# The last batch's second product in seven block products instead of eight, with sums of w_out's blocks made beside four earlier batches

## The chip, the core and the metric

The kernel runs on one core of one Trainium2 chip. The metric is the device time in microseconds of one execution; three executions were timed. The span is the time from the first to the last instruction in the profiled execution.

## What is computed

```python
# per head: q, k, v of (8 batches, 12 heads, 448, 64), fp32
scores = scale * q @ k.T - log(448)
attn   = 1 / (1 + exp(-scores))
x      = (attn @ v) as (8*448, 768)          # heads side by side
# then
h   = x @ w_in                               # 768 x 2048
g   = h - tanh(h)
out = g @ w_out                              # 2048 x 768
```

Everything is fp32 at the edges. Inside, an operand is scaled and split into two fp16 parts (high and low), and a product is three matmuls: high by high, high by low, low by high.

## The kernel before

The program walks over eight batches of 448 tokens, and in each over three kinds of work: attention (`stream`, L506: `scores` L413, sigmoid in `weigh` L434, split in `split_a` L443, times v in `av` L453), the **first product** x @ w_in with the curve g (`moe1`), and the **second product** g @ w_out (`moe2`, L901). PE, ACT, DVE, POOL and, from batch 1 on, SP run in the order in which the program is written. Attention of the next batch is cut into blocks, and `second` (L1161) interleaves them with the second product: a table of positions (`BLOCKS`, `AFTER`, `NORMS7`) says after which step of six matmuls a block, a conversion or a norm comes. All loads and stores go through SP's queue.

Batch 0 also converts the weights, which arrive as fp64 bit patterns: `conv_load` (L154) loads a piece, `conv_sign` and `conv_bits` (L203) make fp32 of it at its `home`, `conv_end` (L207) adds its columns up. w_in comes in 24 pieces, w_out in 32; the last twelve pieces of w_out (the phase "product") are loaded at L172 into tiles `rawo` while the second product of batch 0 already runs. When a half of w_out is there, it is split into fp16 parts in place (`split_w_out`, L334, at L261 to L264).

From batch 3 on (`SEVEN`) the first product is Strassen's: w_in's blocks of 256 x 256 and x's halves are added and subtracted beforehand, and seven products of quarter size take the place of eight (`seven`, L1467: 9 matmuls of 224 columns each, three chunks by three part products). The sums of w_in's blocks were made during batches 1 and 2, lie in DRAM and are streamed through a ring of three buffers (`ring`, `fetch`, L1245). For each k of eight, `Small.moe1` issues `front`, `copy`, `seed`, `cross`, `middle`, `reseed`, `close` and then `square`, `times`, `curve` and `value`, which make g, and `highs` and `lows` (L1452, L1458), which split it. PE does 63 matmuls for a k.

The second product is still the plain one in all batches: for each of three tiles of 128 tokens, 16 chunks of f by three part products by two halves of w_out, 96 matmuls of 384 columns (L921); then the 64 tokens left over, with the two halves side by side in the array (L969, 96 matmuls). ACT and DVE scale the result (L954, L958, L978), and SP stores it (L914). In the last batch no attention is left to interleave.

## Time and profile before

| what | value |
| --- | --- |
| median of 3 runs | 1139.16 us (1138.32 to 1140.37) |
| profiled execution | 1139.2 us |
| its span | 1137.3 us |
| PE busy | 1123.9 us (99%) |
| DVE, ACT, POOL busy | 807.6, 739.7, 216.5 us |
| last batch, first product | from 1028.9 us |
| last batch, second product | from 1079.6 us, with 12 of its matmuls at 1075.9 us |
| last matmul ends | 1132.4 us |

PE, ACT, DVE, POOL and SP are the five instruction queues. "L921" is line 921 of the kernel before. Start times are microseconds from the span's start. PE is busy in all stages; the other engines' shares differ from stage to stage, so what matters is read stage by stage.

### The profile page before, as it was taken

To read this page: it belongs to the slowest core of one execution; us is meant where nothing else is said; L and a number is where in the kernel's file an instruction comes from. 1 tells how busy PE (TensorE), PEld (TensorE's weight loads), DVE (VectorE), ACT (ScalarE), POOL (GpSimd) and SP (SyncE) were. 2 spreads that over 40 slices of the span, in tenths; PEclk is the share of its full clock that TensorE was granted. 3 is DMA by queue.
4 is the path that set the end of the run, shared out by engine and by line. 5 is a ranking of instruction groups with operands and counts; after the bars stand their busy time and mean duration, and the time that the engine had idled before them with its cause. 6 is when DMAs were issued, how large, how long until landed. Compare 5 with 4: busy or idle time off the path is not lost.

```text
span 1137.3 us, 21304 instructions
## 1 busy us (share of the span) xinstructions
PE 1123.9 (99%) x8678; PEld 702.5 (62%) x8678; DVE 807.6 (71%) x1302; ACT 739.7 (65%) x1159; POOL 216.5 (19%) x229
## 2 busy tenths in 40 slices
PE   9999999999999999999999999999999999999998
PEld 2345444555555554569855796559955697559965
DVE  6989699676678787777767686786867777636710
ACT  7987786555886467775676667675676766644610
POOL 0033200014020485310034002320033100330000
PEclk9999999999999999999999999999999999999999
DMA  9992171353222447215622174224622156003301
GB/s 363 404 354 74 29 219 54 83 125 112 75 80 59 141 144 268 73 40 199 236 72 63 51 279 145 63 64 143 246 98 65 43 206 231 17 14 138 128 15 37
DMA packets 64023, 149.28 MB, mean 131 GB/s; under 512 B 18480, under 2 KB 41776, under 8 KB 58800
## 3 DMA queue, kind: packets, MB, share of 16 engines
q1 hardware_dynamic: 63696, 147.55, 38.0%
q8 instruction: 69, 1.13, 0.4%
q10 hardware_dynamic: 224, 0.33, 0.1%
q14 instruction: 34, 0.28, 0.1%
HBM read 119.54 MB, written 28.31 MB: 130 GB/s over the span
## 4 chain that ended last, share of the span: by engine, by line
PE 88%; DMA 4%; DVE 3%; ACT 2%; issue 1%; POOL 1%; SPq 0%; ACTq 0%; DVEq 0%; POOLq 0%
PE po L921 29%; PE ph L1467 16%; PE ph L835 9%; PE acc L463 8%; PE sc L423 8%; PE ph L1047 6%; PE por L969 6%; PE phq L1467 3%; PE php L1467 2%; DMA raw<-moe_w_in 2%; DVE wo L264 1%; ACT a L434 1%; DMA qnn<-q 1%; DVE wi L264 1%; DMA wi<-raw 1%
## 5 line engine op out<-in xcount | busy, mean ns | idle before, releaser
L921 PE MATMUL po<-wo,g 128*128 128x384 f16 x2304 | 389.5, 326 | 1.4 <-DVE g L829 0.7
L921 PEld LDWEIGHTS <-g 128*128 128x128 f16 x2304 | 220.5, 98 | 165.1 <-issue 24.3
L1467 PEld LDWEIGHTS <-wi 128*128 128x128 f16 x2520 | 241.2, 98 | 3.5 <-issue 2.4
L450 DVE SCALAR_TENSOR_TENSOR ahl<-a,ahl 128x896 f16<-128x896 f32 x126 | 156.5, 1254 | 61.7 <-ACT ahl L449 60.3
L434 ACT ACTIVATE a<-sc,nls,rn 128x896 f32<-128x896 f32 x147 | 156.3, 1094 | 50.9 <-PE sc L423 49.5
L1467 PE MATMUL ph<-wi 128*128 128x224 f16 x1890 | 188.5, 259 | 0.1
L494 POOL TENSOR_TENSOR x<-x 128x448 f32<-128x448 f32 x24 | 24.9, 1037 | 488.3 <-ACT x L477 488.3
L835 PE MATMUL ph<-xhl,wi 128*128 128x448 f16 x576 | 109.3, 352 | 0.0
L423 PE MATMUL sc<-Q,K 64*128 64x448 f16 x1008 | 100.8, 353 | 2.4 <-ACT a L434 2.4
L835 PEld LDWEIGHTS <-wi 128*128 128x128 f16 x576 | 56.2, 98 | 52.8 <-issue 0.6
L463 PE MATMUL acc<-ahl,vhl 128*64 128x448 f16 (+1 forms) x864 | 80.6, 356 | 0.0
L449 ACT ACTIVATE ahl<-a 128x896 f16<-128x896 f32 x85 | 79.3, 944 | 0.6
L1047 PE MATMUL ph<-x,wi 128*128 128x448 f32 x192 | 74.5, 541 | 0.0
L423 PEld LDWEIGHTS <-K 64*128 64x128 f16 x1008 | 35.6, 97 | 54.2 <-issue 32.9
L969 PE MATMUL por<-wo,g 128*64 128x384 f16 x768 | 64.9, 327 | 0.0
L463 PEld LDWEIGHTS <-vhl 128*64 128x64 f16 (+1 forms) x864 | 38.4, 108 | 40.2 <-issue 19.8
L1544 ACT ACTIVATE u<-ph,ih 128x896 f32<-128x896 f32 x30 | 30.3, 1009 | 43.7 <-PE ph L1467 43.7
L1047 PEld LDWEIGHTS ph<-x,wi 128*128 128x128 f32 x192 | 35.7, 190 | 33.1 <-issue 31.3
L969 PEld LDWEIGHTS <-g 128*64 128x64 f16 x768 | 42.4, 110 | 22.2 <-issue 4.5
L1458 DVE SCALAR_TENSOR_TENSOR g<-m,Sg,g 128x448 f16<-128x448 f32 x80 | 53.4, 678 | 3.7 <-ACT g L1452 3.7
L958 DVE TENSOR_SCALAR o<-po,iK 128x384 f32<-128x384 f32 x20 | 12.3, 616 | 58.9 <-PE po L921 43.5
L1452 ACT ACTIVATE g<-m,Sg 128x448 f16<-128x448 f32 x80 | 48.9, 660 | 6.9 <-DVE m L1558 5.8
(196 smaller groups left out, 1512.8 us busy)
## 6 DMA issues: line engine op xcount, KB each, us to landing
wi<-set SPq DMA_DIRECT2D x40, 1344.0 KB, 5.9
knn<-k SPq DMA_DIRECT2D x45, 224.0 KB, 2.6
qnn<-q SPq DMA_DIRECT2D x44, 224.0 KB, 2.7
rawo<-moe_w_out SPq DMA_DIRECT2D x22, 384.0 KB, 6.0
out<-o SPq DMA_DIRECT2D x21, 384.0 KB, 2.3
raw<-moe_w_in SPq DMA_DIRECT2D x13, 512.0 KB, 8.1
vn<-v SPq DMA_DIRECT2D x24, 256.0 KB, 3.0
raw<-wi SPq DMA_DIRECT2D x8, 768.0 KB, 8.0
```

The costliest lines, as they stand in the source:

```text
L423: self.nc.tensor.matmul(ps[i * m : (i + 1) * m, h, : self.S], K[i][r, w, c * P : c * P + m], Q[i][r, x, :], start=(n == 0), stop=(n == len ...
L434: self.nc.scalar.activation(a[:, 0], ps[:, :, : self.S], AF.Sigmoid, bias=self.nls, scale=scale)
L449: nc.scalar.activation(A[:, 0], a[:, 0], AF.Copy, scale=A_SCALE)
L450: nc.vector.scalar_tensor_tensor(A[:, 1], a[:, 0], A_SCALE, A[:, 0], op0=ALU.mult, op1=ALU.subtract)
L463: self.nc.tensor.matmul(acc[i][h * D : (h + 1) * D, : self.S], v[k, w, 2 * QT + h if half else h * QT + c], A[k, x, h], start=(n == 0 and ...
L835: self.nc.tensor.matmul(ph, self.wi[:, self.slot(c, k), part, e * P : (e + 1) * P], xhl[c][:, x, :], start=(i == 0), stop=(i == len(prods) ...
L921: nc.tensor.matmul(po[i][:, :H], gs[f // 2][:, x, f % 2, tk * P : (tk + 1) * P], self.wo[:, i * self.NF + 2 * ks[f // 2] + f % 2, w], star ...
L969: nc.tensor.matmul(po[e * D : (e + 1) * D, :H], gs[f // 2][:, x, f % 2, nm:S], self.wo[:, e * self.NF + 2 * ks[f // 2] + f % 2, w], start= ...
L1047: nc.tensor.matmul(ph[:, e, :S], self.fp32(self.wi, self.slot(c, k))[:, 0, e * P : (e + 1) * P], xs[c], start=(c == 0), stop=(c == self.NC ...
L1452: self.nc.scalar.activation(high, src, AF.Copy, scale=self.Sg)
L1458: self.nc.vector.scalar_tensor_tensor(lows[i], srcs[i], self.Sg, highs[i], op0=ALU.mult, op1=ALU.subtract)
L1467: self.nc.tensor.matmul(out, w[:, c, part, left], self.xblock(c, x, right), start=start and i == 0, stop=i == len(prods) - 1, skip_group_c ...
```

## The change

In the last batch (`ACROSS = 7`) the second product is made transposed, out.T = w_out.T @ g.T, and by Strassen's seven products (`across2`). w_out's blocks are the weights, g is what streams, 224 columns (half the tokens) at a time. The six row blocks of 128 of out.T are taken in three pairs; each pair takes seven products, each of eight k by three part products, 24 matmuls. The first matmul of product 1 is 448 columns wide. For k 0 to 4 products 4, 3 and 1 of all pairs come first, then the order of `LAST7`. The result is stored transposed, and the host turns it round.

The operands are sums and differences of blocks:

- of w_out: `conv_end` stores each of the 32 converted pieces to DRAM in batch 0. In batches 3 to 6, 24 units (six in each batch, at the positions of `UNITS7`) each load four fp32 blocks of 128 x 128 of them, make five more by adding (`late_add`, POOL), split all seven (`late_split`, ACT and DVE, on 256 and 640 columns) and store the parts (`late_store`). In the last batch 21 transfers of 512 KB (`late_fetch`) bring them back, 13 before or while the first product ends, eight as places come free.
- of g: `late_sums` makes, for each k, one addition on 448 columns and three on 224; on POOL for k 0 to 6, on DVE for k = 7. `late_parts` splits four blocks (896 columns) and three (672 columns), where `highs` and `lows` split twice 448.

g of the last batch lies where w_out was; the tile of g of the batches before it becomes one tile, `gall`, and takes the fetched sums.

```diff
+    PAIRS = ((0, 1), (3, 4), (2, 5))
+    LAST7 = (
+        (0, 4, ""), (0, 3, "c"), (1, 4, ""), (1, 3, "c"), (0, 1, "s"), (2, 4, ""), (2, 3, "c"), (1, 1, "s"),
+        (0, 5, ""), (2, 1, "s"), (0, 2, "r"), (1, 5, ""), (1, 2, "r"), (0, 7, ""), (0, 6, "po"), (2, 5, ""),
+        (2, 2, "r"), (1, 7, "p"), (2, 7, "p"), (1, 6, "o"), (2, 6, "o"),
+    )
+    LEFT7 = {1: 2, 2: 1, 3: 5, 4: 6, 5: 0, 6: 3, 7: 4}
+    RIGHT7 = {1: 4, 2: 2, 3: 0, 4: 1, 5: 3, 6: 5, 7: 6}
+    FILL7 = 3
+    EXTRA7 = {5: (7, 8), 6: (9, 10)}
+    TAIL7 = (1, 1, 1, 1)
+    BLOCKS7 = (4, 7, 11, 14, 14, 14, 19, 22, 25, 25, 25, 30, 34, 37, 37)
+    LATE = (3, 4, 5, 6)
+    UNITS7 = (2, 5, 7, 10, 13, 15, 18, 22, 25, 29, 31, 34, 38, 41, 45)
...
+    def conv_end(self, p):
+
+        super().conv_end(p)
+        kind, r, i, n = p["piece"]
+        if kind == "out":
+            self.nc.sync.dma_start(
+                self.late_raws[r // 2][:, r % 2, i * n : (i + 1) * n], self.home(kind, r, i)
+            )
...
+    def late_load(self, n, i):
+
+        d, p = divmod(n, self.NB)
+        da, db = self.PAIRS[d]
+        u = n, self.late_home(i)
+        raw = u[1][0]
+        src = self.late_raws[p].rearrange("p f (b n) -> p (f b) n", n=P)
+        self.nc.sync.dma_start(raw[:, 0], src[:, 6 + da])
+        self.nc.sync.dma_start(raw[:, 1], src[:, db])
+        self.nc.sync.dma_start(raw[:, 2:], src[:, da : 6 + db + 1 : 6 + db - da])
+        return u
+
+    def late_add(self, u):
+
+        G = self.nc.gpsimd
+        w, t = u[1][:2]
+        G.tensor_tensor(t[:, :2], w[:, :2], w[:, 2:], op=ALU.add)
+        G.tensor_tensor(t[:, 2], w[:, 2], w[:, 3], op=ALU.add)
+        G.tensor_tensor(t[:, 3], w[:, 1], w[:, 2], op=ALU.subtract)
+        G.tensor_tensor(t[:, 4], w[:, 0], w[:, 3], op=ALU.subtract)
+
+    def late_split(self, u):
+
+        nc = self.nc
+        w, t, high, low = u[1]
+        for src, at in ((w[:, 2:], slice(5, 7)), (t, slice(0, 5))):
+            nc.scalar.activation(high[:, at], src, AF.Copy, scale=self.So)
+            nc.vector.scalar_tensor_tensor(low[:, at], src, self.So, high[:, at], op0=ALU.mult, op1=ALU.subtract)
+
+    def late_store(self, u):
+
+        n, (_, _, *parts) = u
+        d, p = divmod(n, self.NB)
+        for x in range(2):
+            self.nc.sync.dma_start(self.late_sets[d][:, :, p, x], parts[x])
...
+    def late_fetch(self, at):
+
+        if self.late_order:
+            d, n = self.late_order.pop(0)
+            self.late_at[d, n] = at
+            self.nc.sync.dma_start(self.late_ring(at), self.late_sets[d][:, self.LEFT7[n]])
...
+    def late_sums(self, m, G):
+
+        h = self.half
+        t = self.tp.tile([P, 3, h], F32, name="gt", tag="t")
+        q, p = m[:, 0], m[:, 1]
+        G.tensor_tensor(t[:, 1:].rearrange("p b n -> p (b n)"), p, q, op=ALU.add)
+        G.tensor_tensor(t[:, 0], p[:, :h], p[:, h:], op=ALU.add)
+        G.tensor_tensor(q[:, :h], q[:, :h], p[:, h:], op=ALU.subtract)
+        G.tensor_tensor(q[:, h:], q[:, h:], p[:, :h], op=ALU.subtract)
+        return t
+
+    def late_parts(self, m, t, g, which):
+
+        pairs = ((m.rearrange("p a (b n) -> p (a b) n", b=2), slice(0, 4)), (t, slice(4, 7)))
+        for i in which:
+            src, at = pairs[i]
+            self.nc.scalar.activation(g[:, 0, at], src, AF.Copy, scale=self.Sg)
+            self.nc.vector.scalar_tensor_tensor(
+                g[:, 1, at], src, self.Sg, g[:, 0, at], op0=ALU.mult, op1=ALU.subtract
+            )
...
+        def product(d, n, ps=every):
+            q, p = banks[d]
+            out = {1: p[:, :h], 2: q[:, h:], 3: q[:, :h], 4: q[:, h:], 5: q[:, :h], 6: p[:, h:], 7: p[:, :h]}[n]
+            at = self.late_at[d, n]
+            w = self.late_ring(at)
+            right = self.RIGHT7[n]
+            for k in ps:
+                for part, x in ((0, 0), (0, 1), (1, 0)):
+                    start = n in (1, 4) and k == 0 and (part, x) == (0, 0)
+                    wide = 2 if start and n == 1 else 1
+                    nc.tensor.matmul(
+                        p if wide == 2 else out,
+                        w[:, k, part],
+                        gs[k][:, x, right : right + wide],
+                        start=start,
+                        stop=k == self.NB - 1 and (part, x) == (1, 0),
+                        skip_group_check=True,
+                    )
+                count[0] += 1
+                if count[0] % 2 == 0:
+                    yield 1
+            if k == self.NB - 1:
+                self.late_fetch(at)
...
+        def copy(d):
+            sums[d] = c = self.tp.tile([P, 4, h], F32, name="c", tag="t")
+            nc.scalar.activation(c[:, :2].rearrange("p b n -> p (b n)"), banks[d][0], AF.Copy)
+            V.tensor_tensor(c[:, 2], c[:, 0], c[:, 1], op=ALU.add)
+
+        def seed(d):
+            c = sums[d]
+            V.tensor_tensor(c[:, 3], banks[d][1][:, :h], c[:, 2], op=ALU.add)
+
+        def reseed(d):
+            q, p = (t.rearrange("p (b n) -> p b n", b=2) for t in banks[d])
+            V.tensor_tensor(p, sums.pop(d)[:, 3:4].to_broadcast([P, 2, h]), q, op=ALU.subtract)
+            o = self.op.tile([P, 2, h], F32, name="oq", tag="o", bufs=2)
+            nc.scalar.activation(o, q, AF.Copy, scale=iK)
+            rows = self.rows7(d)
+            nc.sync.dma_start(to[rows[0], h:], o[:, 0])
...
+        def out(d, i):
+            o, p = sums[d], banks[d][1]
+            V.tensor_scalar(o[:, i], p[:, i * h : (i + 1) * h], iK, None, op0=ALU.mult)
+            nc.sync.dma_start(to[self.rows7(d)[i], i * h : (i + 1) * h], o[:, i])
+
+        if b + 1 == self.B:
+            for d in range(3):
+                if d:
+                    both = self.ps.tile([P, 2, 512], F32, name="poa", tag="sc", bufs=2)
+                    banks[d] = [both[:, i, : self.S] for i in range(2)]
+                else:
+                    banks[d] = [self.mm(name) for name in ("poq", "pop")]
+                for n in (4, 3, 1):
+                    yield from product(d, n, early)
+            for d, n, after in self.LAST7:
+                yield from product(d, n, rest if n in (4, 3, 1) else every)
+                for f in after:
+                    {"c": copy, "s": seed, "r": reseed, "p": lambda d: out(d, 0), "o": lambda d: out(d, 1)}[f](d)
...
+        def late_tail():
+            square(last)
+            times(last)
+            curve(last)
+            self.late_parts(*rest.pop(last - 2), (1,))
+            value(last)
+            m, g = ms[last][1], self.gs[last]
+            rest[last] = m, self.late_sums(m, V), g
+            for k in (last - 1, last):
+                self.late_parts(*rest[k], (0, 1))
+            yield 1
+            yield 1
 
...
+            m, g = ms[k - 1][1], self.gs[k - 1]
+            if late:
+                rest[k - 1] = m, self.late_sums(m, nc.gpsimd), g
+                if k > 1:
+                    self.late_parts(*rest[k - 2], (0,))
             close(k)
...
+            if late:
+                middle(k + 1)
+                reseed(k + 1)
+                if k > 1:
+                    self.late_parts(*rest.pop(k - 2), (1,))
...
+            if late:
+                self.late_fetch(k - 1)
+                for n in self.EXTRA7.get(k, ()):
+                    self.late_fetch(n)
...
+        if b in self.LATE:
+            n = 3 * self.NB // len(self.LATE)
+            at = (b - self.LATE[0]) * n
+            made = self.late_units(at, at + n)
+            events += [(p, lambda: next(made)) for p in self.UNITS7]```

How the order of the work moves. First DVE in the first product of the last batch, for one k in the steady state; before (`L1515` seed, `L1558` value, `L1550` times, `L1458` the two splits, `L1529` reseed):

```order
L1515 TENSOR_TENSOR ph<-ph,cp 128x224
L1558 SCALAR_TENSOR_TENSOR m<-u,m 128x896
L1550 SCALAR_TENSOR_TENSOR m<-ph,ihk,u 128x896
L1458 SCALAR_TENSOR_TENSOR g<-m,Sg,g 128x448
L1529 TENSOR_TENSOR ph<-cp,ph 128x448
L1458 SCALAR_TENSOR_TENSOR g<-m,Sg,g 128x2x224
```

and now, with the same steps at `L1779`, `L1822`, `L1814` and `L1793`, and `L1407` in `late_parts`:

```order
L1779 TENSOR_TENSOR ph<-ph,cp 128x224
L1822 SCALAR_TENSOR_TENSOR m<-u,m 128x896
L1407 SCALAR_TENSOR_TENSOR wo<-m,Sg,wo 128x896
L1814 SCALAR_TENSOR_TENSOR m<-ph,ihk,u 128x896
L1793 TENSOR_TENSOR ph<-cp,ph 128x448
L1407 SCALAR_TENSOR_TENSOR wo<-gt,Sg,wo 128x672
```

The two splits are wider, the first of them now stands ahead of `times`, and both belong to a k one earlier than before. POOL, which had no work in a first product, now does this for each k there (`late_sums`):

```order
L1395 TENSOR_TENSOR gt<-m 128x448
L1396 TENSOR_TENSOR gt<-m 128x224
L1397 TENSOR_TENSOR m<-m 128x224
L1398 TENSOR_TENSOR m<-m 128x224
```

Between `value` on DVE and the splits two rows later there is now POOL's work. Second, SP's queue in batch 0, where the last pieces of w_out are loaded (`rawo<-moe_w_out`), from the seventh to the twelfth of them; before:

```order
L172 DMA rawo<-moe_w_out 128x384
L357 DMA vn<-v 128x512
L172 DMA rawo<-moe_w_out 128x384 x2
L347 DMA knn<-k 128x448
L172 DMA rawo<-moe_w_out 128x384
L347 DMA qnn<-q 128x448
L357 DMA vn<-v 128x384
L172 DMA rawo<-moe_w_out 128x384 x2
```

and now, with the stores of converted pieces (`late_127<-wo` and so on, L1284):

```order
L173 DMA rawo<-moe_w_out 128x384
L1284 DMA late_127<-wo 128x384
L358 DMA vn<-v 128x512
L1284 DMA late_128<-wo 128x384 x2
L173 DMA rawo<-moe_w_out 128x384 x2
L1284 DMA late_129<-wo 128x384
L348 DMA knn<-k 128x448
L1284 DMA late_129<-wo 128x384
L173 DMA rawo<-moe_w_out 128x384
L348 DMA qnn<-q 128x448
L358 DMA vn<-v 128x384
L173 DMA rawo<-moe_w_out 128x384 x2
```

The tenth load now stands behind the store of the sixth of the twelve pieces (the second of the two `late_129` rows), which waits until DVE has converted that piece.

## Rows read from the trace of the kernel before

**Rows 1.** The page's first lines: the span; of each engine the busy time, its share of the span and its instructions; and GB/s that the DMA engines moved in each of 40 equal slices.

```profile
span 1137.3 us, 21304 instructions
PE 1123.9 (99%) x8678; PEld 702.5 (62%) x8678; DVE 807.6 (71%) x1302; ACT 739.7 (65%) x1159; POOL 216.5 (19%) x229
...
GB/s 363 404 354 74 29 219 54 83 125 112 75 80 59 141 144 268 73 40 199 236 72 63 51 279 145 63 64 143 246 98 65 43 206 231 17 14 138 128 15 37
```

**Rows 2.** All waits of PE for another engine from 430 us to the end: who waited for whom, us in total, times, longest.

```profile
PE sc L423 <- ACT a L434: 1.5, 1, 1.5
```

**Rows 3.** The chain of waits in the last batch (1000 us to the end): start us, us, what. The lines of L1467 are the first product, those of L921 and L969 the second.

```profile
1039.49 0.19 PE php L1496
1049.16 8.62 PE ph L1467 x90
...
1075.90 1.95 PE po L921 x12
...
1079.58 44.85 PE po L921 x276
1124.43 7.94 PE por L969 x96
...
1132.39 0.62 DVE orem L978
```

**Rows 4.** Windows: stretch, length, then busy us (and instructions) of PE, PEld, DVE, ACT and POOL, granted clock, share of the DMA engines, GB/s. The first is the second product of batch 3 with attention of batch 4 in it, the second the first product of batch 7.

```profile
558.60:640.00 81.40, 81.40 (x671) 44.27 (x670) 57.36 (x92) 61.22 (x102) 21.65 (x23) 1.00 0.24 72
...
1028.80:1079.60 50.80, 50.78 (x521) 49.69 (x520) 33.37 (x58) 26.44 (x44) 0.00 (x0) 1.00 0.39 141
```

**Rows 5.** Groups of instructions by line from 900 to 1137 us, shapes kept in the row: line, engine, operation, out<-in, shapes, count | busy us, mean ns of one | idle before.

```profile
L1515 DVE TENSOR_TENSOR ph<-ph,cp 128x224 f32<-128x224 f32 x12 | 4.8, 397 | 6.8 <-ACT cp L1511 6.8
L1558 DVE SCALAR_TENSOR_TENSOR m<-u,m 128x896 f32<-128x896 f32 x16 | 17.5, 1091 | 5.0 <-ACT u L1554 5.0
L1550 DVE SCALAR_TENSOR_TENSOR m<-ph,ihk,u 128x896 f32<-128x896 f32 x12 | 13.8, 1151 | 10.6 <-ACT u L1544 10.6
L1529 DVE TENSOR_TENSOR ph<-cp,ph 128x448 f32<-128x448 f32 x12 | 7.6, 629 | 6.9 <-PE ph L1467 4.2 <-ACT cp L1525 2.7
L1458 DVE SCALAR_TENSOR_TENSOR g<-m,Sg,g 128x448 f16<-128x448 f32 x32 | 21.4, 678 | 1.5 <-ACT g L1452 1.5
L1393 DVE SCALAR_TENSOR_TENSOR wi<-wi,Sx 128x672 f16<-128x672 f32 x3 | 2.7, 914 | 1.0 <-ACT wi L1390 1.0
L1452 ACT ACTIVATE g<-m,Sg 128x448 f16<-128x448 f32 x32 | 19.6, 660 | 2.7 <-DVE m L1558 2.3
L449 ACT ACTIVATE ahl<-a 128x896 f16<-128x896 f32 x11 | 10.4, 946 | 0.1
L1390 ACT ACTIVATE wi<-wi,Sx 128x672 f16<-128x672 f32 x3 | 2.5, 850 | 3.5 <-DVE Sx L757 3.5
L1525 ACT ACTIVATE cp<-ph 128x224 f32<-128x224 f32 x12 | 4.3, 358 | 6.6 <-PE ph L1467 5.6 <-DVE ih L765 1.0
```

**Rows 6.** The timeline of POOL at three places: start us, us, instruction, shapes. At 176.80 us an addition on 448 columns, at 574.80 us one on 224, and at 586.18 us two instructions on 448.

```profile
176.80 1.14 POOL L503 TENSOR_TENSOR x<-x,x 128x448 f32<-128x448 f32 x1 [9.97 <-ACT x L492]
...
574.80 0.65 POOL L1369 TENSOR_TENSOR wi<-x,x 128x224 f32<-128x224 f32 x1
...
586.18 1.10 POOL L494 TENSOR_TENSOR x<-x 128x448 f32<-128x448 f32 x1 [8.27 <-ACT x L477]
587.36 1.87 POOL L503 TENSOR_TENSOR x<-x,x 128x448 f32<-128x448 f32 x1
```

**Rows 7.** The timeline of DVE: two splits in a row that meet those two, and one that meets no work of POOL.

```profile
586.53 3.65 DVE L450 SCALAR_TENSOR_TENSOR ahl<-a,ahl 128x896 f16<-128x896 f32 x2
...
592.16 1.08 DVE L450 SCALAR_TENSOR_TENSOR ahl<-a,ahl 128x896 f16<-128x896 f32 x1
```

**Rows 8.** Batch 0, where the last pieces of w_out come in. The window from 170 to 180 us (columns as in rows 4), two of PE's waits between 30 and 230 us, three rows of SP's timeline, one of DVE's and two of ACT's.

```profile
170.00:180.00 10.00, 10.00 (x69) 4.79 (x68) 9.50 (x23) 9.51 (x18) 1.14 (x1) 1.00 0.24 82
PE po L921 <- DVE g L829: 0.7, 1, 0.7
PE po L921 <- DVE wo L264: 0.6, 1, 0.6
161.89 0.33 SPq L347 DMA_DIRECT2D knn<-k  x1
162.45 0.33 SPq L172 DMA_DIRECT2D rawo<-moe_w_out  x1
164.97 1.99 SPq L172 DMA_DIRECT2D rawo<-moe_w_out  x2
162.76 0.56 DVE L203 SCALAR_TENSOR_TENSOR wo<-rawo,stb 128x384 uint32<-128x384 uint32 x1
166.82 1.01 ACT L187 ACTIVATE stb<-rawo 128x384 f32<-128x384 f32 x2
172.03 0.57 ACT L187 ACTIVATE stb<-rawo 128x384 f32<-128x384 f32 x1 [0.38 <-DMA rawo<-moe_w_out]
```

**Rows 9.** DMA issues over the span: what, queue, count, KB each, median us from issue to landing.

```profile
wi<-set SPq DMA_DIRECT2D x40, 1344.0 KB, 5.9
out<-o SPq DMA_DIRECT2D x21, 384.0 KB, 2.3
set<-wi SPq DMA_DIRECT2D x48, 64.0 KB, 2.0
out<-orem SPq DMA_DIRECT2D x15, 96.0 KB, 2.2
```

More of the change, by code (lines that the diff above doesn't have):

```diff
@@ L47 @@
     SUMS = 1.0
+    ACROSS = 7
     NORMS = (3, 5, 7)
@@ L1483, in moe1 @@
         ix, bound = st
+        late = b >= self.ACROSS
+        rest = {}
+        if late:
+            self.late_at = {}
+            first = [(d, n) for d in range(3) for n in (4, 3, 1)]
+            self.late_order = first + [(d, n) for d, n, _ in self.LAST7 if n not in (4, 3, 1)]
         base = (b - self.SEVEN) * self.NB
```

167 lines of the change are left out of this document (149 added, 18 removed).

## The prediction

> **What bounds the kernel now.** I read the page's first lines, then PE's waits, then the chain of waits of the last batch, then windows of the stages that the change touches, and at the end single instructions. The page shows PE busy for 1123.9 of 1137.3 us [rows 1], and PE's waits say that this is no average over good and bad stages: from 430 us to the end PE waited for another engine once, for 1.5 us [rows 2]. The chain of the last batch accordingly runs through PE alone, apart from the last two instructions: the first product, then 288 matmuls of 384 columns, then 96 of the rest [rows 3]. So in the last batch time is PE's columns, and a change is worth what it takes off PE, less what it makes PE wait. Batch 0 is the exception: from 170 to 180 us DVE and ACT are both busy for 95% of the time, and PE waits for them (0.7 and 0.6 us are two such waits) [rows 8]. There the conversion of w_out sets the pace, and whatever delays it can come out at the end.
>
> The sum is made against the profiled execution, 1139.2 us, which stands 0.04 us above the median of the runs. About 0.2% of it, 2.3 us, is what a measurement of this kernel tells from no change.
>
> **What the change takes off PE.** Removed: 1.95 + 44.85 + 7.94 = 54.74 us [rows 3]. Added: three pairs by seven products by eight k by three part products, 504 matmuls of 224 columns with 128 x 128 fp16 weights. The first product runs just that shape: 90 in a row took 8.62 us, 95.8 ns each [rows 3]. 504 x 95.8 ns = 48.28 us. Three of them are 448 columns wide; such a one took 0.19 us [rows 3], so 3 x 0.094 = 0.28 us more, 48.56 us in all. **Saved: 6.18 us.** Seven eighths would have given 6.8 us; the short matmuls give part of it back, though the rest of 64 tokens was already dear.
>
> **The end.** After the last matmul DVE scaled 384 columns in 0.62 us [rows 3]; now it is 224 columns, for which a read of PSUM took 0.40 us [rows 5]. Saved: 0.22 us. The last store is 112 KB; stores of 96 and 384 KB landed in 2.2 and 2.3 us [rows 9], so nothing changes there.
>
> **The last batch's first product: DVE and ACT.** PE spends 63 x 95.8 ns = 6.04 us on a k. DVE's work for it was seed 0.40, value 1.09, times 1.15, reseed 0.63 and two splits of 0.68 [rows 5], 4.63 us. The splits become one of 896 columns, 1.08 us when POOL is quiet [rows 7], and one of 672, 0.91 us [rows 5]: 5.26 us, still under 6.04. ACT's two splits go from 1.32 us to 0.95 + 0.85 = 1.80 us [rows 5]; ACT was busy for 26.44 of 50.80 us there [rows 4], and eight times 0.48 us is 3.8 us more. Neither would bind. The order also helps: the wide split now stands ahead of times, and behind times only reseed is left before close of the next k needs it.
>
> **The last batch's first product: POOL.** This is the term that I trust least. POOL did nothing in a first product (0.00 us) [rows 4]; now it adds 448 columns once (1.14 us) and 224 three times (0.65 us) [rows 6] for each k, 3.09 us. POOL and DVE get in each other's way: at 586 us two DVE splits that take 1.08 us alone took 3.65 us together while POOL ran, and POOL's addition of 448 columns, which starts at 587.36 us among them, took 1.87 instead of 1.14 us [rows 6, 7]. 1.10 us of POOL, 1.08 of DVE, 1.14 of POOL and 1.08 of DVE, one behind the other, make 4.4 us, and from 586.18 to 590.18 us 4.0 passed: they took turns, with some overlap at each change. Which of DVE's instructions are met so these rows do not say, so I bound it. If all five groups are met, DVE needs 5.26 + 3.09 = 8.35 us for a k, 2.31 over PE's time, and over seven k that is 16.2 us; that end is the rival below. If only the three that read two tiles of SBUF are met, as the split at 586 us does (value 1.09, splits 1.08 and 0.91), the turns add to 3.08 + 3.09 = 6.17 us against 6.04: just full, and with the overlap at each change just under. times, seed and reseed read PSUM on one side. Below zero it can't go, since nothing is taken away there. I take **0.5 us**, near the second case: what is met at 586 us is an instruction that reads SBUF twice.
>
> The Trainium skill has a rule here that speaks against this change (SBUF — State Buffer, section "SBUF: two separate sides"): the pair of SBUF ports that DVE and GpSimd share is a lock for a whole instruction, and besides 2-port modes it is a DVE instruction with two SBUF inputs that takes it. The rows at 586 us agree as far as they go (3.65 us for two that take 1.08 alone). By the rule alone, with no overlap at the changes, 7 x (6.17 - 6.04) = 0.9 us would stand in the place of the 0.5.
>
> **The seam between the products.** g of k = 7 comes from late_tail behind close. Its DVE work after the last close: times 1.15, a split 0.91, value 1.09, the sums of k = 7 (one 448 and three 224 columns, at most 0.63 + 3 x 0.40 by the nearest additions), four splits 2 x (1.08 + 0.91) [rows 5, 7], together 8.9 us, and about 1 us before them on ACT. PE has 117 of its 135 early matmuls for it, 11.2 us, and reads the second half of k = 7 only some 45 matmuls later. No charge. The 13 places fetched ahead hold 13 x 0.5 = 6.8 MB; with the 141 GB/s of that stage [rows 4] this makes some 275 GB/s, where a slice of this trace moved 404 [rows 1]. A transfer of 1344 KB lands in 5.9 us [rows 9]; the eight refills have over 10 us each. No charge.
>
> **Batches 3 to 6.** A unit costs ACT about 0.36 + 0.85 us and DVE 0.40 + 0.91 (by the rows of 224 and 672 columns, for 256 and 640) [rows 5], POOL at most 4 x 0.65. Six units: ACT 61.22 + 7.3 = 68.5 of 81.40 us, DVE 57.36 + 7.9 = 65.2, POOL 21.65 + 15.6 = 37.3 [rows 4]. The DMA engines were busy for 24% and get 4.2 MB more in 81 us. The two ends are nothing and all of DVE's work, 4 x 7.9 = 31 us. I take **nothing**: PE has not one wait there [rows 2] while DVE and ACT idle for 24 and 20 us. If that cover is gone at a few places, the rival below gives the price.
>
> **Batch 0.** 32 stores go into SP's queue. Where the conversion sets the pace, the tenth of the last twelve loads went out at 162.45 us; it now stands behind the store of a piece whose DVE instruction starts at 162.76 and takes 0.56 us [rows 8]. With 0.4 us for the store's issue that is 163.7 us, 1.3 us later. ACT starts on this piece at about 167.3 us (the second of the two at 166.82) [rows 8], 4.8 us after the old issue, so ACT waits about as long as the load is late, and all behind it with it. The next pair goes out at 164.97 us, after that; its last piece was already waited for (0.38 us) [rows 8]. Ends: nothing, if DVE's queue has enough to do meanwhile, and twice the delay, 2.6 us, if the store traffic slows the loads as well. I take **1.0 us**, most of one delay, since both engines are 95% busy.
>
> **The sum.** 1139.2 - 6.18 - 0.22 + 0.5 + 0 + 1.0 = **1134.3 us**.
>
> **Rivals.** (a) The forecast, between 1132.8 (no charge) and 1135.5: for it speaks that PE is the only bound in the last batch and that every price is of the same shape in the same kernel. Chance 0.60. (b) Both charges larger: 2.6 us in batch 0 and about 1 to 3 us of POOL's turns: 1136.4 to 1138.4. For it: both places are full by the sums above. Chance 0.17, most of it still faster than 1136.9. (c) **Slower:** POOL's sums hold DVE up in all it does, the first product of the last batch becomes DVE's: 8.35 us for a k, 16.2 us in all, 1139.2 - 6.4 + 1.0 + 16.2 = 1150.0 us. It decides from the point where DVE's time for a k passes 6.04 + 5.4 / 7 = 6.81 us, that is 1.55 us of waiting for a k. Against it: only one kind of instruction is seen to wait. Chance 0.07. (d) The units' work hits attention in batches 3 to 6: if one in four of the 24 units puts its DVE time of 1.31 us on PE, 7.9 us, 1142.2 us. Against it: the idle time above. Chance 0.09. (e) The change does not bring what it says: weights come late, or the matmuls run slower than in the first product (at 108.6 ns each, 54.74 / 504, nothing is left). One transfer of up to 5.9 us in the open gives 1140.2. Chance 0.07.
>
> **How the numbers follow.** The time is that of (a). The range 1132.2 to 1140.2 us goes half a microsecond below the case without charges, and up to (e); it holds (a), (b) and (e), 0.84, and leaves out (c) and (d). Faster by over 0.2% (below 1136.9): (a) and most of (b), 0.74. Within 0.2%: the rest of (b) and half of (e), 0.10. Slower: (c), (d) and a little of (e), 0.16.
>
> **What would show it.** PE's second product in the last batch as 504 matmuls in 48.6 us without a wait; one k of the first product still 6.04 us, with DVE at 87% or more and POOL at half; POOL's additions stretched, and value and the splits too, but not times; no new wait of PE in batches 3 to 6; in batch 0 the second product's end some 1 us later. I am wrong if PE waits in the last batch's first product for reseed (close late), or if 224 columns take more than 96 ns.

## The result: slower, 1145.28 against 1139.16 us

The changed kernel takes 1145.28 us (1144.22 to 1146.15, five runs), the kernel before 1139.16 us: ratio 1.0053, 95% interval 1.0038 to 1.0068. Forecast were 1134.3 us and a gain. The profiled execution took 1144.22 us. Its page, first lines (columns as in [rows 1]), and all waits of PE from 430 us on (as in [rows 2]):

```profile
span 1142.3 us, 22173 instructions
PE 1119.9 (98%) x8798; PEld 720.3 (63%) x8798; DVE 886.7 (78%) x1368; ACT 769.4 (67%) x1210; POOL 345.1 (30%) x353
```

```profile
PE po L925 <- DVE o L962: 3.9, 6, 0.9
PE acc L464 <- ACT tn L376: 3.7, 3, 1.2
PE sc L424 <- ACT a L435: 1.0, 1, 1.0
PE por L973 <- ACT o L958: 1.0, 3, 0.3
```

PE has less to do than before (1119.9 us against 1123.9) and waits more. The `sc` wait comes ahead of batch 3 and stood there before; the other three rows are 8.6 us, and the rest of the loss below is in gaps that this view does not list. Where it arises, the starts of the first products tell, in the two profiles:

| stage | before | after | difference | forecast |
| --- | --- | --- | --- | --- |
| to the first product of batch 3 | 507.80 | 508.58 | +0.78 | +1.0 |
| batches 3 to 6 | 520.99 | 531.41 | **+10.42** | 0 |
| batch 7, to its last matmul's end | 103.6 | 97.7 | -5.9 | -5.7 |
| behind it | 5.0 | 4.7 | -0.3 | -0.2 |

Batch by batch the 10.42 us are 3.23, 2.98, 2.86 and 1.35, all of it in the second products. The windows of the same work in the second product of batch 3, before and after, and of the first product of batch 7, after (columns as in [rows 4]):

```profile
560.90:639.80 78.90, 78.90 (x655) 42.67 (x654) 55.93 (x90) 58.84 (x99) 21.65 (x23) 1.00 0.23 71
561.80:643.80 82.00, 79.24 (x655) 43.61 (x653) 71.40 (x102) 64.74 (x110) 45.99 (x47) 1.00 0.44 120
...
1040.00:1090.40 50.40, 50.38 (x526) 50.13 (x525) 36.22 (x55) 27.98 (x43) 25.19 (x24) 1.00 0.69 256
```

DVE was busy for 55.9 us before, now for 71.4: 15.5 us more where 7.9 were forecast. POOL was busy for 24.3 us more, where at most 15.6 were forecast. In batch 7 the view of waits lists none for PE. What happens in batch 3, on three engines; the first fence is the timeline of DVE, the second POOL's, the third PE's (start us, us, instruction):

```profile
573.14 1.22 DVE L451 SCALAR_TENSOR_TENSOR ahl<-a,ahl 128x896 f16<-128x896 f32 x1
574.57 1.53 DVE L451 SCALAR_TENSOR_TENSOR ahl<-a,ahl 128x896 f16<-128x896 f32 x1 [0.21 <-ACT ahl L450]
576.08 1.29 DVE L1339 SCALAR_TENSOR_TENSOR lo<-wi,so,wo 128x256 f16<-128x256 f32 x1
577.30 1.28 DVE L1339 SCALAR_TENSOR_TENSOR lo<-wo,so 128x640 f16<-128x640 f32 x1
578.50 0.60 DVE L962 TENSOR_SCALAR o<-po,iK 128x384 f32<-128x384 f32 x1
```

```profile
572.58 0.83 POOL L1331 TENSOR_TENSOR wo<-wi 128x128 f32<-128x128 f32 x1
573.78 1.38 POOL L495 TENSOR_TENSOR x<-x 128x448 f32<-128x448 f32 x1 [0.36 <-ACT x L478]
575.23 1.86 POOL L504 TENSOR_TENSOR x<-x,x 128x448 f32<-128x448 f32 x1
577.06 0.83 POOL L1626 TENSOR_TENSOR wi<-x,x 128x224 f32<-128x224 f32 x1
```

```profile
578.26 0.34 PE L925 MATMUL po<-wo,g 128*128 128x384 f16 x1
579.16 3.90 PE L925 MATMUL po<-wo,g 128*128 128x384 f16 x23 [0.56 <-DVE o L962]
```

PE can go on with the next tile of 128 tokens only when DVE has read the old one (`o`). A unit's two splits, at place 15, stand just ahead of `o` in DVE's queue. Alone they take 0.48 and 0.88 us; here 1.29 and 1.28, and `ahl` (attention's split) ahead of them 1.22 and 1.53 instead of 1.08, because POOL works almost without a pause from 567.14 to 582.24 us, first on two units' additions, then on the sums of x. The sums of x alone, which were there before, are most of the splits' stretch: in x1 below, without the units' additions, the same two took 2.10 us together (574.82 us on DVE), here 2.50. Over batches 3 to 6 the units' splits took 3.6 us more than in x1, the instructions of `ahl` 18 us more.

The second kind of wait starts on POOL; `tn` is a step of the next head's norms. ACT's timeline:

```profile
607.24 0.49 ACT L1338 ACTIVATE wi<-wi,so 128x256 f16<-128x256 f32 x1
610.33 0.83 ACT L1338 ACTIVATE wi<-wi,so 128x640 f16<-128x640 f32 x1 [2.59 <-POOL wi L1331]
611.06 0.25 ACT L376 ACTIVATE tn<-pbn,tiny 128x6 f32<-128x6 f32 x1
```

The wide split of the fifth unit waits 2.59 us for POOL's additions, which stand behind five sums of x; `tn` stands behind the split, attention behind `tn`, and PE waits 1.24 us for it at 611.36 us.

### The profile page after: what moved, and what is told of

Its sections match the earlier page's. It is cut to its first block, busy times and chain, and to the rows that moved or that the text cites. A ratio compares the mean times of both kernels' runs of the same rounds, so it can differ in the third digit from the quotient of the medians.

```text
span 1142.3 us, 22173 instructions
## 1 busy us (share of the span) xinstructions
PE 1119.9 (98%) x8798; PEld 720.3 (63%) x8798; DVE 886.7 (78%) x1368; ACT 769.4 (67%) x1210; POOL 345.1 (30%) x353
## 3 DMA queue, kind: packets, MB, share of 16 engines
q8 instruction: 70, 1.15, 0.4%
## 5 line engine op out<-in xcount | busy, mean ns | idle before, releaser
L925 PE MATMUL po<-wo,g 128*128 128x384 f16 x2016 | 343.6, 326 | 5.5 <-DVE o L962 3.9
L925 PEld LDWEIGHTS <-g 128*128 128x128 f16 x2016 | 192.3, 98 | 152.0 <-issue 30.1
L451 DVE SCALAR_TENSOR_TENSOR ahl<-a,ahl 128x896 f16<-128x896 f32 x126 | 166.6, 1339 | 41.7 <-ACT ahl L450 40.2
L435 ACT ACTIVATE a<-sc,nls,rn 128x896 f32<-128x896 f32 x147 | 155.8, 1090 | 38.2 <-PE sc L424 36.8
L424 PE MATMUL sc<-Q,K 64*128 64x448 f16 x1008 | 101.0, 353 | 3.3 <-ACT a L435 3.3
L1328 POOL TENSOR_TENSOR wi<-wi 128x256 f32<-128x256 f32 x12 | 12.2, 1018 | 285.0 <-DMA wi<-late 212.4
L464 PE MATMUL acc<-ahl,vhl 128*64 128x448 f16 (+1 forms) x864 | 80.6, 356 | 3.7 <-ACT tn L376 3.7
L450 ACT ACTIVATE ahl<-a 128x896 f16<-128x896 f32 x85 | 79.2, 943 | 0.6
L424 PEld LDWEIGHTS <-K 64*128 64x128 f16 x1008 | 35.6, 97 | 55.2 <-issue 33.4
L464 PEld LDWEIGHTS <-vhl 128*64 128x64 f16 (+1 forms) x864 | 39.3, 108 | 43.2 <-issue 23.3
L495 POOL TENSOR_TENSOR x<-x 128x448 f32<-128x448 f32 x24 | 27.7, 1155 | 115.7 <-ACT x L478 115.7
L973 PE MATMUL por<-wo,g 128*64 128x384 f16 x672 | 56.9, 327 | 1.0 <-ACT o L958 1.0
L1808 ACT ACTIVATE u<-ph,ih 128x896 f32<-128x896 f32 x30 | 30.2, 1005 | 40.1 <-PE ph L1724 40.1
L1814 DVE SCALAR_TENSOR_TENSOR m<-ph,ihk,u 128x896 f32<-128x896 f32 x30 | 34.5, 1150 | 23.2 <-ACT u L1808 23.2
L1822 DVE SCALAR_TENSOR_TENSOR m<-u,m 128x896 f32<-128x896 f32 x40 | 44.1, 1102 | 10.1 <-ACT u L1818 10.0
L1676 POOL TENSOR_TENSOR wsq<-wsq 128x768 bf16<-128x768 bf16 (+1 forms) x16 | 20.7, 1295 | 101.0 <-PE wl L219 60.1
## 6 DMA issues: line engine op xcount, KB each, us to landing
wi<-set SPq DMA_DIRECT2D x40, 1344.0 KB, 5.9
rawo<-moe_w_out SPq DMA_DIRECT2D x22, 384.0 KB, 5.4
out<-o SPq DMA_DIRECT2D x18, 384.0 KB, 2.4
```

The lines of the kernel that those rows point to most:

```text
L424: self.nc.tensor.matmul(ps[i * m : (i + 1) * m, h, : self.S], K[i][r, w, c * P : c * P + m], Q[i][r, x, :], start=(n == 0), stop=(n == len ...
L435: self.nc.scalar.activation(a[:, 0], ps[:, :, : self.S], AF.Sigmoid, bias=self.nls, scale=scale)
L450: nc.scalar.activation(A[:, 0], a[:, 0], AF.Copy, scale=A_SCALE)
L451: nc.vector.scalar_tensor_tensor(A[:, 1], a[:, 0], A_SCALE, A[:, 0], op0=ALU.mult, op1=ALU.subtract)
L464: self.nc.tensor.matmul(acc[i][h * D : (h + 1) * D, : self.S], v[k, w, 2 * QT + h if half else h * QT + c], A[k, x, h], start=(n == 0 and ...
L925: nc.tensor.matmul(po[i][:, :H], gs[f // 2][:, x, f % 2, tk * P : (tk + 1) * P], self.wo[:, i * self.NF + 2 * ks[f // 2] + f % 2, w], star ...
```

## The experiments

The excess below is that of batches 3 to 6 over the 520.99 us of before, from the starts of the first products in each kernel's profile. Of six kernels there is one execution only; for them the excess and the waits carry the argument, and not the time.

| kernel | us | ratio, 95% interval | excess |
| --- | --- | --- | --- |
| changed | 1145.28 | 1.0053 (1.0038 to 1.0068) | 10.4 |
| x1, no sums | 1132.82 | one execution | 0.0 |
| x2, no DVE split | 1134.09 | one execution | 0.9 |
| x3, neither | 1134.26 | one execution | 1.1 |
| x6, sums unread | 1139.70 | one execution | 7.0 |
| x5, no sums, split twice | 1169.92 | one execution | 36.1 |
| y1, sums on DVE | 1167.67 | one execution | 33.5 |
| x4, moved | 1151.64 | 1.0119 (1.0090 to 1.0147) | 16.0 |
| y5, three early | 1148.12 | 1.0074 (1.0061 to 1.0087) | 14.1 |
| z1, y5 without stores | 1148.25 | 1.0067 (1.0054 to 1.0080) | 15.9 |
| z2, y5, POOL's queue | 1147.67 | 1.0068 (1.0055 to 1.0081) | 15.0 |
| w1, two early | 1156.92 | 1.0158 (1.0137 to 1.0178) | 23.7 |
| w2, two early, old places | 1160.50 | 1.0178 (1.0164 to 1.0192) | 27.6 |
| w3, seven in batch 6 | 1162.95 | 1.0215 (1.0201 to 1.0229) | 28.1 |
| w4, stores later | 1141.03 | 1.0013 (1.0003 to 1.0023) | 8.1 |
| w5, split at 28 | 1143.93 | 1.0036 (1.0023 to 1.0048) | 9.8 |
| w6, decoupled | 1139.36 | 1.0005 (0.9996 to 1.0014) | 6.5 |
| w7, decoupled, 36 | 1139.89 | 1.0006 (0.9997 to 1.0016) | 6.0 |
| w8, additions at 28 | 1142.03 | 1.0024 (1.0014 to 1.0033) | 9.3 |

**Which work of a unit costs.** x1:

```diff
 def late_add(self, u):
-    (POOL's four additions)
+    pass
 ...
-for src, at in ((w[:, 2:], slice(5, 7)), (t, slice(0, 5))):
+for src, at in ((w[:, 2:], slice(5, 7)), (w[:, 2:3].to_broadcast([P, 5, P]), slice(0, 5))):
```

> The changed kernel without POOL's additions in the units of batches 3 to 6: the wide split reads one loaded block five times over instead of the five sums, so loads, splits and stores are as before and what is stored is not the sums. The changed kernel's batches 3 to 6 (from the start of one first product to the next) are together 10.4 us longer than before (135.2, 135.0, 134.8 and 126.4 us against three times 132.0 and 125.1). Theory A (POOL's additions and DVE's instructions take turns, and that is what makes DVE late): the excess falls below 2 us, PE's waits for o on DVE and for tn on ACT go, DVE's split of ahl is back at about 1.24 us from 1.37; time about 1136. Theory B (the splits alone overfill DVE): the waits for o stay, about 4 us, and only the three waits of 1.2 us for tn behind an ACT split that waits for POOL go; excess 5 to 7 us, time about 1141. Theory C (traffic of the loads and stores): nothing changes, 1145.

x2 leaves out the line of `nc.vector` in `late_split` and stores `parts[0]` twice; x3 does both.

> The changed kernel without the two DVE splits of each unit; the high parts are stored in the place of the low ones. POOL's additions, ACT's splits, loads and stores stay. Theory A: the additions still stretch attention's own instructions on DVE (17 us over batches 3 to 6 for the two kinds of ahl alone) and still come late for ACT, so the three waits for tn stay (3.7 us) and some of those for o; excess 4 to 6 us, time about 1140. Theory B: with 43 us of DVE work gone the waits for o go and only those for tn stay; excess 4 us or less, time about 1139. Theory C: nothing changes, 1145.

> The changed kernel with neither the additions nor the DVE splits in the units; ACT's splits, loads and stores stay, and what is stored is not the sums. Theories A and B: batches 3 to 6 take what they took before (excess under 1 us), the time is about 1135, and what is left against 1134.3 is batch 0's. Theory C: as the changed kernel, 1145.

x1 is as theory A has it: batches 3 to 6 take 520.98 us, and PE does not wait in them. But x2, where A expected 4 to 6 us, comes out at 0.9 (0.8 of it a wait for a late `wi`, a transfer of the ring). So neither A nor B alone: either half of a unit's cost fits, both together don't. Of traffic (C) no more than such late transfers is seen. The second product of batch 3, window in x1, then in x2, and the two splits of x1 ahead of `o`:

```profile
560.80:639.70 78.90, 78.90 (x655) 42.70 (x654) 65.38 (x102) 65.30 (x111) 25.33 (x23) 1.00 0.46 126
561.40:640.30 78.90, 78.90 (x655) 42.73 (x654) 60.26 (x90) 65.49 (x111) 39.95 (x47) 1.00 0.46 126
574.82 2.10 DVE L1334 SCALAR_TENSOR_TENSOR lo<-wi,so,wo 128x256 f16<-128x256 f32 x2 [0.37 <-ACT wo L1333]
```

DVE's busy time goes from 55.9 (before) over 65.4 (x1, no wait) to 71.4 us (changed): 9.5 us are the splits, 6.0 us are POOL's additions showing up in DVE's time (4.3 us without the splits, in x2). x5 asks whether the source matters. On top of x1:

```diff
-            nc.vector.scalar_tensor_tensor(low[:, at], ...)
+            for _ in range(2):
+                nc.vector.scalar_tensor_tensor(low[:, at], ...)
```

> As the kernel without sums (POOL's additions left out, the wide split reads a loaded block), but each DVE split of a unit is issued twice, so that what is stored is not the sums: DVE gets some 36 us more over batches 3 to 6, as much as it loses by POOL's turns and by the stretched splits in the changed kernel (65 - 36 = 29 us, by busy time). If DVE's time just ahead of o is what counts, from whatever source, PE waits for o again, 0.5 to 1.5 us at the places 16 and 32, and batches 3 to 6 take 4 to 12 us more than before: 1137 to 1145. If POOL's turns and late sums themselves are needed, no wait comes back: 1133 to 1135.

The waits for `o` came back far larger, 3.2 and 2.6 us at the two places of each batch (DVE's timeline, then PE's; the four splits are one row):

```profile
577.38 4.07 DVE L1335 SCALAR_TENSOR_TENSOR lo<-wi,so,wo 128x256 f16<-128x256 f32 x4
581.38 0.60 DVE L962 TENSOR_SCALAR o<-po,iK 128x384 f32<-128x384 f32 x1
```

```profile
582.04 5.21 PE L925 MATMUL po<-wo,g 128*128 128x384 f16 x23 [3.17 <-DVE o L962]
```

So DVE's time ahead of `o` is enough, without POOL's additions. It is more time than theirs, though: over batches 3 to 6 DVE was busy for 370.4 us before, 408.8 in x1, 436.7 in the changed kernel and 454.8 here, 46.0 us over x1 where the additions make it 27.9. The excess is three times the upper end of what was expected. Part of that is PE's clock: behind six of the eight waits it fell (23 matmuls take 5.21 us here, 3.90 in the changed kernel's row above).

x6 keeps POOL's additions, but the splits read as in x1:

> The changed kernel with POOL's additions made as before, but the wide split reads a loaded block five times over, so that nobody waits for the sums and what is stored is not the sums. It parts the two ways in which the additions can cost: that they take turns with DVE (the waits for o stay, 0.5 to 0.9 us at two places of each batch, about 4 us in all), and that ACT's split waits for them with tn behind it (1.2 us in each of three batches, which goes here). Both at work: 1137 to 1141. Turns alone: still 1142 or more. Lateness alone: 1133 to 1135.

Both at work: the waits for `tn` are gone, those for `o` stay, and the excess is 7.0. By difference, from one profile each, 7.0 of the 10.4 us are POOL's turns with DVE, 3.4 us ACT's wait for late sums. PE's waits in x6:

```profile
PE po L925 <- DVE o L962: 4.0, 4, 1.2
PE por L973 <- ACT o L958: 1.1, 3, 0.4
```

These are 5.1 us; the other 1.9 us is in gaps that this view does not list. y1 takes POOL out of it (`G = self.nc.vector` in `late_add`):

> The changed kernel with the units' sums on DVE instead of POOL: about 0.35 + 3 x 0.17 = 0.86 us for a unit, 21 us in all (worked out from 0.62 us for 448 and 0.30 us for 224 columns on DVE in the last batch's late_tail), in the place of POOL's additions with their turns. If DVE's sum of work decides, wherever it comes from, DVE gains 21 us and loses about 25 us of stretch, and the excess of batches 3 to 6 stays at 5 to 10 us: 1141 to 1145. If it is the turns and POOL's lateness alone, the waits go as without the sums: 1133 to 1136.

DVE's sum of work decides, and it is worse than expected: the excess is 33.5 us. The additions were priced at 0.35 and 0.17 us; they take 0.42 and 0.28 us on DVE alone and 0.66 to 0.75 us beside POOL's sums of x in batch 3 (577.96 to 580.62 us), and they stand ahead of the splits and `o`. PE waits 24.0 us for `o`, in eight places.

**Whether other places have room.** x4:

```diff
-    UNITS7 = (2, 5, 7, 10, 13, 15, 18, 22, 25, 29, 31, 34, 38, 41, 45)
+    UNITS7 = (2, 5, 7, 10, 13, 17, 18, 22, 25, 33, 34, 38, 40, 43, 45)
```

> The changed kernel with six of the fifteen places of the units' steps moved (15 to 17, 29 to 33, 31 to 34, 34 to 38, 38 to 40, 41 to 43): the splits that stand ahead of DVE's o in its queue come behind it, and the split behind which ACT's tn waits for POOL's additions comes four steps of six matmuls later. If the order in the queues is what counts, the waits for o (3.9 us in sum) and for tn (3.7 us) go, and the time is 1138 to 1140. If DVE has no room left in those stretches, the same work makes attention late instead: PE waits for acc or sc, and the time stays within 2 us of 1145.

The waits for `o` and `tn` went and larger ones came: 1.84 us for `m` of the next batch's norms, behind the splits moved to 38 and 43, 1.35 us at `por` and 0.4 to 0.6 us for `ahl`. DVE has no room at the end of this stage in batches 3 to 5; in batch 6 the same places cost only 0.3 us. y5 moves three units of each batch into its first product, one after the other, a step (load, add, split and store) at the end of each k; z1 and z2 are y5 with `conv_end`'s stores left out and on POOL's queue:

> The changed kernel with three of each batch's six units moved from the second product into the first product of the same batch, one after the other in the home that lies outside x's parts (late_home(1)), a step at the end of each k; the other three keep the first nine places of the table. Each first product gets POOL's twelve additions and six DVE splits, about 5 us of each, where DVE was busy for 33 of 51 us. If the excess of batches 3 to 6 is POOL's additions and DVE's splits meeting attention where DVE has no room, the waits at the places 31 and 34 go and one wait for o of 0.2 to 0.6 us a batch may stay: 1134 to 1136, about 10 us under the changed kernel. Rival: the chain of close, square, times and reseed of the first product is as full, and PE waits there for reseed, 1140 or more.

> The kernel with three units in the first product, without the 32 stores of converted pieces in batch 0; the units load w_in's blocks, which lie in DRAM anyway, so the sums are of other blocks. If the stores in SP's queue hold up the last loads of w_out (1.0 us in the prediction; batch 1's first product began 1.3 us later than before), this is 0.7 to 1.3 us faster than the same kernel with the stores. If batch 0's delay is of another source, or given back later, the two are the same within 0.4 us.

> The kernel with three units in the first product, with the 32 stores issued from POOL's queue instead of SP's. If only SP's order counts, this is as fast as without the stores. If the traffic counts, as slow as with them. POOL issues the stores with waits for DVE in its own queue, where it also adds up attention's x; if that gets late, it is slower than either.

y5 is the rival: in the first product of batches 3 to 6 attention of the next batch fills DVE at k = 1 to 4, and PE waited eight times for `seed` (6.0 us), behind the splits at k = 2 and 4; the unit at k = 6 cost nothing. The three units left in the second product still made PE wait for `o`, 3.4 us in four places. In batch 0 the profiles show the stores: batch 1's first product starts at 226.1 us on average in nine profiles with them on SP, at 225.0 without (225.05 before, 225.04 in z1, one profile each), at 225.4 with POOL's queue (nine profiles, one of them at 227.5). The times of y5, z1 and z2 can't tell 1 us apart: their intervals overlap.

w1, w2 and w3 use what y5 showed: two units in each first product where attention is not (one split ahead of `close(0)`, one behind k = 6), the rest in the second product, the stores on POOL's queue.

> The changed kernel with POOL's queue for the 32 stores of batch 0 (1.1 us by the profiles: batch 1's first product began at 224.9 instead of 226.1), two units of each batch in the first product where it has no attention block beside it (one split ahead of close(0), one behind k = 6) and four in the second product, with the split that stood ahead of o moved behind it (15 to 17, 29 to 33 and 36). Waits left by the run with moved places: 0.35 and 0.63 us for ahl in each batch; those for tn and for seed go. 1134 to 1137. If DVE is too full whatever the places, waits of the old size come back elsewhere: 1139 or more.

> As the kernel before it in this list, but the four units in the second product keep the changed kernel's first eleven places (15, 29 and 31 among them). The waits for o (0.56 and 0.65 us in batch 3 of the changed kernel) stay and that for tn goes: 1135 to 1138, and as fast as the moved places within 1.5 us.

> Two units in each first product as in the kernels before, but only three in the second products of batches 3 to 5 and seven in that of batch 6, where DVE was busy for 42 of 72 us before. With three units at the places up to 25 no more than one wait of 0.4 us in each of three batches, and in batch 6 one or two for o of up to 1 us: 1133 to 1136. If the seven meet in batch 6, 2 to 4 us more.

All three share one fault. The early unit's store and the next unit's loads stand in SP's queue ahead of the ring's next transfer (SP's timeline of w1, then PE's):

```profile
655.39 1.19 SPq L1352 DMA_DIRECT2D lates<-lo  x1
...
658.30 12.80 SPq L1523 DMA_DIRECT2D wi<-set  x3
```

```profile
664.37 3.54 PE L1745 MATMUL ph<-wi 128*128 128x224 f16 x18 [3.17 <-DMA wi<-set]
```

In the changed kernel that transfer was issued at 654.51 us. Four such waits were 13.4 us, and behind three of them PE ran at half its clock (1.2 GHz) for some 3 to 6 us; behind the first, 3.19 us at 528.09 us, it did not (window of w1 behind the second, granted clock 0.50):

```profile
664.00:668.00 4.00, 3.63 (x20) 2.88 (x21) 0.46 (x1) 0.00 (x0) 0.00 (x0) 0.50 0.67 285
```

w2's old places brought back 5.4 us of waits for `o`. w3 shows besides that seven units don't fit into the second product of batch 6: of 13.8 us of excess in that batch 5.1 are a wait for `wi`, 3.4 are waits for `o`. And it shows that three do fit: the second products of batches 3, 4 and 5 take 0.03, 0.00 and 0.00 us longer than before (window of w3 in batch 3, PE busy throughout):

```profile
561.80:644.80 83.00, 83.00 (x687) 45.97 (x685) 67.67 (x101) 64.62 (x109) 35.51 (x35) 1.00 0.37 105
```

w4 stores a step later, w5 moves the third split and the fourth unit's additions from 22 to 28:

> As the kernel with two units in the first product and moved places, but each of those two is stored a step later (behind k = 1, and at place 1 of the second product), so that the store's wait for the split does not stand ahead of the ring's next transfer in SP's queue: there PE waited 13.4 us in four places for wi (3 to 4 us each, with half the granted clock for some 4 us behind each). Those go, 0.4 to 0.8 us for ahl in each batch stay: 1133 to 1137, faster than before the change. If the first product has no room for a unit in any place, PE waits there for seed or wi as before: 1140 or more.

> As the kernel before it in this list, with the third split and the fourth unit's additions at place 28 in the place of 22, behind the stretch in which DVE has no idle time (582 to 594 us in the second product of batch 3 before the change). If it is that stretch which makes ahl late, the wait of 0.4 to 0.8 us for ahl goes: 0.5 to 2.5 us faster than the kernel before it in this list. If additions and split then meet o of the second tile instead, a wait of like size comes there and the two are the same within 1 us.

w4 lost the waits for `wi` but for one of 0.6 us, and kept one for `ahl` of 1.0 to 1.6 us in each batch. In w5 that is 0.3 us or nothing, and PE waits 1.8 us for `tn` instead, in three batches. w6 gives additions and splits places of their own, w7 moves w6's last split to 36, w8 moves w7's last additions back to 28:

```diff
+    STEPS7 = (
+        (2, "l", 0), (5, "a", 0), (7, "l", 1), (10, "s", 0), (10, "a", 1), (13, "t", 0), (13, "l", 2),
+        (17, "a", 2), (17, "s", 1), (18, "t", 1), (18, "l", 3), (22, "a", 3), (28, "s", 2), (29, "t", 2), (33, "s", 3), (34, "t", 3),
+    )
```

> Two units in each first product and four in the second, as in the two kernels before, but with additions and splits in places of their own: the fourth unit's additions at 22, ahead of the sums of x in POOL's queue at 25 (they stood behind them at 28, and ACT's tn waited 1.8 us behind a split that waited for them), the third split at 28, behind the stretch where DVE has no idle time, the fourth at 33; in the first product additions at k = 5 in the place of 4. Left over then are waits of 0.3 us for ahl: 1134 to 1137, faster than before the change by 2 to 5 us. Rival: three of four splits in the second half of a tile are as late for o as they were: waits for o of 0.5 to 1 us in each batch and 1138 to 1141.

> As the kernel before it in this list, with the fourth split at 36 in the place of 33, behind tn in ACT's queue. If tn still waits behind this split in the kernel before, this is 1 to 3 us faster; if DVE's full stretch in the third tile makes ahl late for it, PE waits 0.5 to 1 us there in each batch and this is 1 to 4 us slower.

> As the kernel with the fourth split at 36, with the fourth unit's additions at 28 in the place of 22. In the kernel with them at 22 they ran at 590.2 to 594.4 us of its trace, beside vhl and ahl on DVE, and PE waited 1.0 to 1.4 us for ahl in each batch, its only wait there; with them at 28 (and the split at 33) that wait was 0.3 us and tn's 1.8 us, and with the split at 36 no tn waited. If both hold together, 3 to 4 us less than the kernel before: 1135 to 1137, faster than before the change. If the additions behind the sums of x now stretch ahl and o of the second tile instead, a wait of like size comes there and the time stays at 1138 to 1141.

w6 and w7 are as fast as before the change and not faster. Their one wait left in a second product is 1.0 to 1.4 us for `ahl` (PE's waits of w6 from 200 us on, then POOL's timeline and DVE's):

```profile
PE acc L464 <- DVE ahl L451: 4.7, 4, 1.4
```

```profile
590.25 1.11 POOL L1332 TENSOR_TENSOR wo<-wi 128x256 f32<-128x256 f32 x1
...
593.85 0.57 POOL L1335 TENSOR_TENSOR wo<-wi 128x128 f32<-128x128 f32 x1
```

```profile
590.82 2.76 DVE L451 SCALAR_TENSOR_TENSOR ahl<-a,ahl 128x896 f16<-128x896 f32 x2
```

In w8, with the additions behind the sums of x, that wait is 0.3 us in batch 3 and 0.6 in batch 6, so it was the additions. But there the last split waits 2.5 us for them (609.13 us on ACT) and PE 1.8 us for `tn` in three batches: place 36 is still ahead of `tn` in ACT's queue, which I had taken the other way round. The additions are late at 28 and in DVE's way at 22; four units in a second product have no free place among those tried. Three have one (w3), two have one in a first product (in w7 the first products of batches 3 to 6 are as long as before), and in batch 6 six cost 0.3 us (x4): with two in each first product and three, three, three and six in the second ones that would be 23 of the 24 units. These were not run together.

## Why the prediction was wrong

**The step that failed** is "Batches 3 to 6 ... I take nothing". Its sum of work was about right for the splits alone (0.48 + 0.88 = 1.36 us a unit on DVE, 1.31 forecast), but it left out what POOL's sums do to DVE, while the prediction itself priced POOL's turns in batch 7. With them DVE grew by 15.5 us in batch 3, not 7.9: 9.5 us for the splits and 6.0 for the additions' turns. And it held the average idle time of 24 us against it, though DVE has its idle time in pieces of 1 to 2.4 us ahead of `o` (DVE's timeline of before), and from 582 to 593.8 us none:

```profile
572.76 1.09 DVE L450 SCALAR_TENSOR_TENSOR ahl<-a,ahl 128x896 f16<-128x896 f32 x1 [1.01 <-ACT ahl L449]
576.23 0.62 DVE L958 TENSOR_SCALAR o<-po,iK 128x384 f32<-128x384 f32 x1 [2.38 <-PE po L921]
578.04 0.63 DVE L447 TENSOR_SCALAR ahl<-a 128x896 f16<-128x896 f32 x1 [1.19 <-ACT a L434]
```

x1 and x5 show both: without the additions the splits fit, with more DVE time at the same places they don't. Rival (d), 7.9 us and 1142.2, was this case in kind, at a chance of 0.09; the range ended at 1140.2 because it was left out.

Two smaller slips of the prediction did not decide. It counted most of rival (b) as faster than 1136.9 us, though only a quarter of its stretch from 1136.4 to 1138.4 lies below that, so 0.74 for a gain was too high by its own numbers. And the rest of 64 tokens was not dear: 7.94 us, against 7.80 for half a tile of the others.

A second wait was not seen: a split on ACT that waits for POOL, with `tn` behind it (3.4 us by x6). The prediction counted POOL's 37.3 of 81.4 us and not what its queue has ahead of the additions.

**What held, and by what luck.** Batch 7 came out at -5.9 us against -6.18 + 0.5, but by two misses that nearly cancel. The 0.5 us for POOL's turns did not come, and 0.3 of the 6.18 us are missing. Of these, 0.27 us are lost in the seam, which had been given no charge: PE waits there for DVE's split of g of k = 7, and 18 matmuls take 2.16 us instead of 1.89 (PE's timeline). POOL's turns fell on the instructions that the prediction named (groups by line, 1040 us to the end, as in [rows 5]):

```profile
1101.89 2.16 PE L1436 MATMUL poq<-wo,g 128*128 128x224 f16 x18
...
L1395 POOL TENSOR_TENSOR gt<-m 128x448 f32<-128x448 f32 x7 | 12.1, 1729 | 35.0 <-DVE m L1822 35.0
L1407 DVE SCALAR_TENSOR_TENSOR wo<-m,Sg,wo 128x896 f16<-128x896 f32 x8 | 10.0, 1251 | 0.2 <-ACT wo L1406 0.2
L1822 DVE SCALAR_TENSOR_TENSOR m<-u,m 128x896 f32<-128x896 f32 x8 | 9.2, 1144 | 3.2 <-ACT u L1818 3.2
L1407 DVE SCALAR_TENSOR_TENSOR wo<-gt,Sg,wo 128x672 f16<-128x672 f32 x8 | 7.6, 953 | 2.4 <-ACT wo L1406 1.9
L1814 DVE SCALAR_TENSOR_TENSOR m<-ph,ihk,u 128x896 f32<-128x896 f32 x6 | 6.9, 1145 | 2.4 <-ACT u L1808 2.4
```

The addition of 448 columns took 1.73 us instead of 1.14 and the wide split 1.25 instead of 1.08, while `times`, which reads PSUM, kept its 1.15 us: rival (c) was rightly put aside. But the turns were priced far too high for DVE. `value` and the two splits became 0.26 us a k longer together, where turns with all of POOL's work would have made it 3.09; POOL's own additions became 1.2 us a k longer. DVE was busy for 72% of the first product (36.22 of 50.40 us), not for 87% or more, POOL for half, as forecast. A k still took 6.04 us. Batch 0 cost 1.29 us at batch 1's first product and 0.78 at batch 3's, against 1.0; over the profiles the stores are worth about 1.0, within a scatter of 0.5 us. The tail's gain of 0.3 us proves nothing: in the profiles of the changed kernels it takes 4.2 to 5.5 us.

## What to carry to other kernels

Idle time counts at the place where an in-order queue has it, ahead of the instruction that a full engine waits for, and not as a sum over the stage; list what stands in the queue ahead of each such instruction. In this kernel POOL's work was also work on DVE, 6.0 us in the second product of batch 3 and 0.26 us in a k of batch 7, so price it on both, stage by stage. When added work makes a stage wait, drop its parts one at a time, and put them back one at a time: that either half fits says nothing of the whole.
